# Four attention layers on one core: a new order of work, one product of 320 keys, smaller helpers

## The chip, the core and the metric

The kernel runs on one core of a Trainium2 chip. Its time is the device time of one execution in microseconds (us); of several runs the median is given. The core has five queues of instructions that run beside each other: TensorE (matrix products), VectorE, ScalarE, GpSimd and SyncE, which only issues transfers (DMAs). In the profile they are PE (PEld for its weight loads), DVE, ACT, POOL and SP. ScalarE's queue can issue DMAs too.

## The reference

2048 tokens of 512 values pass through four layers A, B, A, B. Each normalizes its input, projects it to queries, keys and values of 32 heads with 16 values each, attends, projects with `wo` and adds the input.

```python
# layer A: each token attends to 8 keys, 2 tokens apart
idx = pos[:, None] - (jnp.arange(8) * 2)[None, :]
logits = where(idx >= 0, einsum("bhsd,bhswd->bhsw", q, kg) * scale, -1e9)
o = einsum("bhsw,bhswd->bhsd", softmax(logits), vg)
# layer B: each token attends to the 256 tokens that end with itself
mask = (i - j >= 0) & (i - j < 256)
p = softmax(where(mask, einsum("bhqd,bhkd->bhqk", q, k) * scale, -1e9))
o = einsum("bhqk,bhkd->bhqd", p, v)
# between layers
x = x + A(layernorm(x)); x = x + B(layernorm(x)); ...   # twice
```

## The kernel before, in words

Tokens go through in 8 chunks of 256 per layer, and a chunk of a layer starts as soon as the chunk of the layer below has ended. Matrix products split float32 numbers into two halves of 16 bits (high and low) and add three products (L1037 to L1039 for products that come out transposed, L1057 to L1060 for the others).

**Weights.** `prep` loads each weight matrix, sums its squares, and forms a power of two as its scale: the sums are reduced over columns (`most`, L871), transposed by TensorE, reduced again and worked into factors on one partition (`one`, L880 to L886), and spread to 128 partitions by a second product (`spreads`, L893). ScalarE and VectorE then split the weights with it.

**Layer A.** Scores of the local window come from 128 small products (L1196), go to DRAM and back as bands (`shelve`, `band`), become weights by a softmax on VectorE, ScalarE and GpSimd, pass through DRAM again (`put`, `get` into `ptt`), and meet the values, which were read with a shift (`window`), in small products (L1305).

**Layer B.** Queries and keys are written to DRAM as high and low halves and read back into stacks, 48 partitions of high, low and high halves for two groups of heads (`stack`, L1358). `stk[hf, 0]` holds queries; `stk[hf, 1]` and `stk[hf, 2]` hold the keys of two chunks in turn. In every chunk but a layer's first, one step of `halves` (L1416) makes the scores of 128 queries of one column of heads against the 320 keys that can matter, for the row maxima: four positions in the array, and for each the keys of the chunk before (`bef`) and of this one (`now`) in a product of their own, 8 products and 8 weight loads. VectorE picks and reduces (L1435, L1431), the maxima go through DRAM into the query stack as two more rows (`mput`, `mget`), and the scores are formed again with keys as rows (L1567), raised by ScalarE (L1577, L1589), masked by GpSimd or VectorE (L1606, L1600) and multiplied with the values (L1622), which carry a column of ones so that the sum of the weights comes along. In all chunks but the last, the sums are gathered, inverted and spread by DMAs. In the last chunk (`final`), TensorE spreads each head group's sums over partitions (`across`, L1653), VectorE inverts 128×256 of them (L1657) and multiplies (L1658).

**The order.** Nothing here is left to run time. `plan.add` notes each task with an engine, a cost, what it reads and writes and, for some, another engine (`alt`). The table `ORDER` gives every task its place in its engine's queue; a negative entry puts it on the other engine. `Plan.order` merges the five queues into one program by its model of costs and delays, and so also chooses the memory banks of TensorE's results. The model holds a clock for TensorE (`RECENT`, `WARM`), a delay for its instruction supply (`SUPPLY`), and a price for leaving one kind of TensorE work for another (`mode`, `LEAVE`): F are projections, Q the steps of L1416 and L1567, X, V, C and R the other small products. 122 warm-up blocks of three products (L1752, scope "W") have places too. A queue runs in order: an instruction that waits holds up all behind it.

## Time and profile before

| | |
|---|---|
| Median of 3 runs | 1435.89 us (1431.45 to 1438.87) |
| The profiled execution's own time | 1437.16 us, span 1435.4 us |
| TensorE: busy, products | 1306.9 us, 28226 |
| VectorE, ScalarE, GpSimd: busy | 867.4, 824.0, 392.8 us |
| DMA: moved, packets | 195.20 MB, 185233 |

The span runs from the first to the last instruction. Busy time is the time in which at least one instruction of an engine is under way; products overlap, so a product's own duration is longer than its share of the engine. A row of waits reads: engine, line, what it waited for, then the total in us, the number of times and the longest. A row of a timeline reads: start, duration, engine, line, operation, number of instructions merged into it, and in brackets the idle time of that engine before it with what ended it. A row of a stretch of time gives for each engine its busy time and, in brackets, its number of instructions, then TensorE's granted clock (1.00 is full) and the busy share of the DMA engines.

### The profile page before, as it was taken

How to read it: one execution, taken by the hardware profiler on the slowest of the kernel's cores; microseconds unless marked ns; L12 is line 12 of the kernel's file. 1: busy time of each engine (PE TensorE's matmuls, PEld its weight loads, DVE VectorE, ACT ScalarE, POOL GpSimd, SP SyncE). 2: the span in 40 equal slices, each digit the busy share in tenths (PEclk: the TensorE clock that was granted, in tenths of full speed). 3: DMA queues.
4: the chain of work that ended last, by engine and by line, in shares of the span. 5: the costliest groups of instructions: out<-in, count | busy, mean ns of one | idle time of the engine just before them, and what ended most of it. 6: DMA issues, size and time to landing. Idle time of an engine off the chain costs nothing.

```text
span 1435.4 us, 64450 instructions
## 1 busy us (share of the span) xinstructions
PE 1306.9 (91%) x28226; PEld 861.9 (60%) x28226; DVE 867.4 (60%) x1942; ACT 824.0 (57%) x1298; POOL 392.8 (27%) x841
## 2 busy tenths in 40 slices
PE   9999999898999989989998989979988798998987
PEld 7775566574665747547564646647565474664643
DVE  5646764755657385555845548574753656658596
ACT  8555666374755656546583646637565364654643
POOL 4221232222432142132332322423323222212040
PEclk9999999899999999999999999989999899999999
DMA  9765555737355463645538364463636535354322
GB/s 301 210 169 143 139 112 153 160 99 170 84 167 125 125 161 98 156 119 146 117 103 191 97 189 130 149 149 97 157 78 175 122 110 158 85 154 109 103 61 68
DMA packets 185233, 195.20 MB, mean 136 GB/s; under 512 B 92892, under 2 KB 123356, under 8 KB 184952
## 3 DMA queue, kind: packets, MB, share of 16 engines
q1 hardware_dynamic: 155772, 163.27, 43.0%
q10 hardware_dynamic: 29180, 27.82, 7.5%
q8 instruction: 221, 3.62, 1.1%
q14 instruction: 60, 0.49, 0.1%
HBM read 94.11 MB, written 79.36 MB: 121 GB/s over the span
## 4 chain that ended last, share of the span: by engine, by line
PE 65%; DMA 12%; DVE 7%; issue 5%; ACT 4%; SPq 4%; ACTq 2%; POOL 1%; DVEq 0%; POOLq 0%
PE banks L1037 7%; PE banks L1622 7%; PE banks L1038 7%; PE banks L1039 6%; PE banks L1059 6%; PE banks L1057 6%; PE banks L1060 5%; PE banks L1567 4%; PE banks L1416 4%; PE banks L1305 3%; PE banks L1196 3%; DVE m L1431 2%; PE banks L1752 2%; DMA stk<-re 2%; DMA re<-eh 1%
## 5 line engine op out<-in xcount | busy, mean ns | idle before, releaser
L1431 DVE TENSOR_REDUCE m<-banks 128x2 f32<-128x512 f32 x448 | 302.0, 689 | 8.4
L1577 ACT ACTIVATE p<-banks,sclB 128x896 f32<-128x896 f32 x224 | 220.9, 1008 | 62.1 <-PE banks L1567 48.0
L1435 DVE COPY_PREDICATED banks<-trm,banks 128x128 f32<-128x128 int16 x448 | 124.5, 291 | 143.1 <-PE banks L1416 127.6
L1606 POOL TENSOR_SCALAR_AFFINE_SELECT p<-p 64x256 f32<-64x256 f32 x292 | 114.2, 413 | 277.8 <-ACT p L1577 262.8
L1606 POOL TENSOR_SCALAR_AFFINE_SELECT ps<-ps 64x256 f32<-64x256 f32 x280 | 109.7, 414 | 260.4 <-ACT ps L1589 219.0
L1416 PE MATMUL banks<-stk,stk 48*64 48x256 f16 (+3 forms) x3584 | 139.2, 246 | 36.3 <-DVE m L1431 10.0
L1416 PEld LDWEIGHTS <-stk 48*64 48x64 f16 x3584 | 79.0, 109 | 113.2 <-issue 95.8
L1567 PE MATMUL banks<-stk,stk 64*64 64x128 f16 (+3 forms) x3584 | 120.9, 242 | 20.4 <-DMA stk<-md 3.7
L1589 ACT ACTIVATE ps<-banks,sclB 128x768 f32<-128x768 f32 x112 | 100.5, 902 | 46.7 <-PE banks L1567 21.4
L1622 PE MATMUL banks<-p,v 64*32 64x192 f32 (+1 forms) x3584 | 114.8, 360 | 5.7 <-issue 1.6
L1567 PEld LDWEIGHTS <-stk 64*64 64x64 f16 x3584 | 70.7, 109 | 74.0 <-issue 64.1
L1337 DVE SCALAR_TENSOR_TENSOR el<-banks,eh 128x512 f16<-128x512 f32 x64 | 42.8, 689 | 99.9 <-ACT eh L1334 88.1
L1205 ACT COPY s<-banks 128x624 f32<-128x624 f32 x64 | 75.1, 1263 | 44.9 <-PE banks L1196 39.5
L1639 ACT COPY os<-banks 128x256 f32<-128x256 f32 x112 | 41.1, 375 | 81.2 <-PE banks L1622 62.8
L1636 DVE TENSOR_TENSOR os<-os,banks 128x256 f32<-128x256 f32 x112 | 45.8, 416 | 69.0 <-ACT os L1639 65.9
L1622 PEld LDWEIGHTS banks<-p,v 64*32 64x32 f32 x3584 | 65.4, 107 | 32.4 <-issue 16.0
L1622 PE MATMUL banks<-ps,v 64*32 64x64 f32 (+1 forms) x3584 | 69.2, 246 | 8.5 <-issue 8.5
L1305 PE MATMUL banks<-ptt,vs 39*32 39x64 f32 x4096 | 58.9, 247 | 17.7 <-DMA ptt<-ptd 6.8
L1037 PE MATMUL banks<-xh,wA0h 128*128 128x256 f16 x256 | 71.5, 279 | 1.8 <-DMA xh<-ht 1.8
L1622 PEld LDWEIGHTS banks<-ps,v 64*32 64x32 f32 x3584 | 64.6, 106 | 13.5 <-issue 12.0
L1037 PE MATMUL banks<-xh,wA1h 128*128 128x256 f16 x256 | 71.2, 278 | 0.4 <-DMA xh<-ht 0.2
L1038 PE MATMUL banks<-xl,wA0h 128*128 128x256 f16 x256 | 70.9, 277 | 0.0
(215 smaller groups left out, 3096.9 us busy)
## 6 DMA issues: line engine op xcount, KB each, us to landing
sd<-s SPq DMA_DIRECT2D x128, 156.0 KB
stk<-re SPq DMA_DIRECT2D x188, 96.0 KB
ptt<-ptd SPq DMA_DIRECT2D x124, 96.0 KB
re<-eh SPq DMA_DIRECT2D x80, 128.0 KB
vd<-ve SPq DMA_DIRECT2D x32, 256.0 KB
xm<-y SPq DMA_DIRECT2D x32, 256.0 KB
y<-xm SPq DMA_DIRECT2D x32, 256.0 KB
vs<-vd ACTq DMA_DIRECT2D x44, 156.0 KB
```

The costliest lines, as they stand in the source:

```text
L1037: nc.tensor.matmul(ps[mp].t[:, i], wh, xh, start=k == 0, stop=False)
L1038: nc.tensor.matmul(ps[mp].t[:, i], wh, xl, start=False, stop=False)
L1039: nc.tensor.matmul(ps[mp].t[:, i], wl, xh, start=False, stop=k == 3)
L1305: nc.tensor.matmul(acc.t[32 * r : 32 * r + 32, bb].rearrange("p (a x q u) -> p a x q u", a=2, q=16, u=2)[:, :, 2 * m + b2], vs.t[k, b2, 32 ...
L1416: nc.tensor.matmul(o, lhs, k, start=True, stop=True, tile_position=(64 * par, 64 * h))
L1431: nc.vector.tensor_reduce(out=m.t[:, :, u, qb], in_=ps.t[:, :, 0 : 2 * P], op=ALU.max, axis=AX.X)
L1435: nc.vector.copy_predicated(t[:, :, 0:64], trm[:, 0].bitcast(I16).unsqueeze(1).broadcast_to([P, 2, 64]), t[:, :, C : C + 64])
L1567: nc.tensor.matmul(ps.t[64 * h : 64 * h + 64, par, at + x0 : at + x0 + q1 - q0], stk[hf, kt][r, col, k0 : k0 + 64], stk[hf, 0][r, col, q0: ...
L1577: nc.scalar.activation(big.t[:, 2 * i : 2 * i + 2], ps.t[:, :, 0:448], AF.Exp, scale=scl["B", 1])
L1589: nc.scalar.activation(small.t.rearrange("p (i m) x -> p m i x", i=2), ps.t[:, :, 0:384].rearrange("p m (i x) -> p m i x", i=2), AF.Exp, s ...
L1606: E.affine_select(out=v, in_=v, pattern=[[0, 4], [a, 64]], compare_op=op, fill=0.0, base=0, channel_multiplier=-a)
L1622: nc.tensor.matmul(acc.t[32 * mm : 32 * mm + 32, h, q0:q1], vv[r, 17 * (H * blk + hd) : 17 * (H * blk + hd) + 32], x.t[r, mm, x0 : x0 + q1 ...
```

## The change

- All lists of `ORDER` are new. Few tasks keep their places. Counted over the lists, TensorE's queue changes its mode 1145 times (1011 before).
- The model of the planner: TensorE's clock is set by activity in four staggered grids of 3.4133 us, its activity numbers are others, `SUPPLY` and `SLACK` are larger and the supply is asked for one after the other, and some DMA costs are higher. The model reaches the program through the merging and the banks.
- `band`, `window`, `get`, `stack`, `mget` and `spread` have no other engine any more: 80 such issues leave ScalarE's queue. Of the others, ScalarE's queue takes 30 more net (`mput` 6, `gather` 6, `gather_o` 8, `shelve` 7, `put` 3). In all, its issues go from 181 to 131.
- By the lists, VectorE takes 90 masks (81), 10 subtractions `rest` (4), 10 scalings of `oc` (3) and 8 differences `less` (13).
- The key stacks of two chunks lie in one tile, `ring`, chunk beside chunk. In odd chunks the 320 keys lie in a row, and `halves` needs 4 products and 4 weight loads a step. In even chunks it has 8 as before. The transfers into key stacks now write pieces of 512 bytes; the DRAM tensor `re` has its axes in another order.
- The weight scale: the sums of squares are multiplied by a matrix of ones, so that each partition has their total, and five small VectorE operations make the factors in place. The scale comes from the total and not from the largest.
- The last chunk's division: products bring the sums to a tile of 128×8, VectorE inverts that, ScalarE spreads it, products turn it back, and VectorE multiplies from the bank.

```diff
-RECENT, WARM, EDGE = 3.4, 0.31, 0.05
-SLACK = 0.6, 0.25
-SUPPLY = 4.2
+GRID, LOW, EDGE = 3.4133, 0.4, 0.03
+SLACK = 0.9, 0.45
+SUPPLY = 5.0
...
-    stk, vst = {}, {}
+    stk, vst, ring = {}, {}, {}
     for hf in range(2):
+        stk[hf, 0] = cst.tile([P, 8, C], F16, name=f"stk{hf}_q")
+        ring[hf] = cst.tile([P, 8, 2, C], F16, name=f"stk{hf}_k")
         for i in range(3):
-            stk[hf, i] = cst.tile([P, 8, C], F16, name=f"stk{hf}_{i}")
+            if i:
+                stk[hf, i] = ring[hf][:, :, i - 1]
...
-            def most(am=am, ax=ax, n=n):
-                nc.vector.tensor_reduce(out=ax.t[:, 0:n], in_=am.t[:, 0:n], op=ALU.max, axis=AX.X)
...
-            plan.add("DVE", 1.0 if n == 1 else 1.2, one, r=[vpt], w=[va])
-            plan.add("PE", 0.3, spreads, r=[va, vone], w=[vpb])
...
+            def total(pt=pt, am=am, n=n):
+                for j in range(2):
+                    nc.tensor.matmul(pt.t[:, 0:n], ones.t.rearrange("p a b -> p (a b)")[:, 0:P], am.t[:, 0:n, j], start=j == 0, stop=j == 1)
+
+            plan.add("PE", 0.3, total, r=[*vam, vone], w=[vpt], rec=8)
+
+            def factors(some=some, pt=pt, a1=a1, n=n):
+                a, b = a1.t[:, 0:n], pscs[T, some]
+                nc.vector.tensor_scalar(a, pt.t[:, 0:n], 2.0 ** -120, 2.0 ** 120, op0=ALU.max, op1=ALU.min)
+                nc.vector.tensor_scalar(a.bitcast(I32), a.bitcast(I32), 1, 0x7F800000,
                                         op0=ALU.logical_shift_right, op1=ALU.bitwise_and)
+                nc.vector.tensor_scalar(b[:, :, 0], a, 2.0 ** 64, None, op0=ALU.mult)
+                nc.vector.tensor_scalar(a, a, 2.0 ** 64 / WS, None, op0=ALU.mult)
+                nc.vector.reciprocal(b[:, :, 1], a)
...
-            plan.add("SP", 2.15, shelve, r=vS, w=[vsd], size=600, alt=("ACT", 2.4))
-            plan.add("SP", 0.65, band, r=[vsd], w=[vL[t]], size=160, alt=("ACT", 0.7))
+            plan.add("SP", 2.4, shelve, r=vS, w=[vsd], size=600, alt=("ACT", 2.4))
+            plan.add("SP", 0.65, band, r=[vsd], w=[vL[t]], size=160)
...
                     for par in range(2):
-                        E.dma_start(t[64 * par : 64 * par + 48, 4 * hp : 4 * hp + 4].rearrange("p a t -> p (a t)"), src[j, par])
-
-                plan.add("SP", 1.3, stack, r=vre[0] + vre[1], w=[vst[hf, i, hp]], size=192, alt=("ACT", 1.35))
+                        x = t[64 * par : 64 * par + 48, 4 * hp : 4 * hp + 4]
+                        if s == 0:
+                            E.dma_start(x.rearrange("p a t -> p (a t)"), src[j, par])
+                        else:
+                            E.dma_start(x, src[j, par].rearrange("p (a t) -> p a t", a=4))
+
+                plan.add("SP", 1.3, stack, r=vre[0] + vre[1], w=[vst[hf, i, hp]], size=225 if s else 192)
...
-                        for part in range(2):
+                        for part in range(2 - c % 2):
                             for h in range(2):
                                 for par in range(2):
                                     r = slice(64 * par, 64 * par + 48)
                                     n = C - qb * P - 64 * h
                                     lhs = stk[hf, 0][r, col, qb * P + 64 * h : qb * P + 64 * h + 64]
                                     o = ps.t[64 * h : 64 * h + 64, par, 0:320]
-                                    o, k = (o[:, 0:n], stk[hf, bef][r, col, C - n :]) if part == 0 else (o[:, n:], stk[hf, now][r, col, : 320 - n])
+                                    if c % 2:
+                                        k = ring[hf][r, col].rearrange("p i t -> p (i t)")[:, C - n : C - n + 320]
+                                    else:
+                                        o, k = (o[:, 0:n], stk[hf, bef][r, col, C - n :]) if part == 0 else (o[:, n:], stk[hf, now][r, col, : 320 - n])
                                     nc.tensor.matmul(o, lhs, k, start=True, stop=True, tile_position=(64 * par, 64 * h))
...
-                def divide(pb=pb, sh=sh, some=some):
-                    nc.vector.reciprocal(sh.t[:, 0:C], pb.t[:, 0:C])
-                    nc.vector.tensor_mul(some(), some(), sh.t[:, 0:C])
...
+                def sums(pb=pb, some=some):
+                    for b in range(2):
+                        nc.tensor.matmul(pb.t[:, C + 4 * b : C + 4 * b + 4], some()[:, b * P : (b + 1) * P], idf[:, 16::32], start=True, stop=True)
+
+                def wide(r8=r8, sh=sh):
+                    nc.scalar.copy(sh.t[:, 0:C].rearrange("p (b m x) -> p b m x", b=2, m=4),
+                                   r8.t.rearrange("p (b m) -> p b m", b=2).unsqueeze(3).broadcast_to([P, 2, 4, 32]))
+
+                def back(pb=pb, sh=sh):
+                    for b in range(2):
+                        nc.tensor.matmul(pb.t[:, b * P : (b + 1) * P], sh.t[:, b * P : (b + 1) * P], idf, start=True, stop=True)
+
+                plan.add("PE", 0.3, sums, r=[vsm], w=[vps], mode="F", act=0.02, rec=8)
+                plan.add("DVE", 0.16, lambda pb=pb, r8=r8: nc.vector.reciprocal(r8.t, pb.t[:, C : C + 8]), r=[vps], w=[vr8])
+                plan.add("ACT", 0.3, wide, r=[vr8], w=[vbr])
+                plan.add("PE", 0.47, back, r=[vbr], w=[vpb], mode="F", act=0.42, rec=8)
```

More of the change, by code (lines that the diff above doesn't have):

```diff
@@ L568, in order, with cool @@
         slow, at, rest = None, 0.0, 0.0
-        dma, mode, tail, use, since = 0.0, "", "", 0.0, 0.0
-        n, asked, told = 3, 0.0, 0.0
+        dma, mode = 0.0, ""
+        heat = [[0.0, GRID * (k + 1) / 4, 0.0] for k in range(4)]
+        n, asked, told, mark = 3, 0.0, 0.0, 0.0
         out = []
+        def cool(h):
+            h[2] = 1.0 / (1.0 + math.exp((h[0] / GRID - LOW) / EDGE))
+            h[0] = 0.0
+            h[1] += GRID
         def begins(e):
@@ L634, in order @@
                 mode = t.mode
-                use *= math.exp((since - now) / RECENT)
-                clock = 0.5 + 0.5 / (1.0 + math.exp((WARM - use) / EDGE))
-                a = t.act / us * clock
-                us /= clock
+                for h in heat:
+                    while h[1] <= now:
+                        cool(h)
+                us /= 1.0 - sum(h[2] for h in heat) / 8
                 wait = 0.0
                 for x in range(n + 1, n + t.rec + 1):
-                    if x % 256 == 140:
-                        asked, told = told, now + wait + us * (x - n) / t.rec
+                    if x % 256 == 152:
+                        mark = now + wait + us * (x - n) / t.rec
+                    elif x % 256 == 168:
+                        asked, told = told, max(mark, now, told + SUPPLY if told else 0.0)
                     elif x % 256 == 193 and x > 256:
@@ L646, in order @@
                 us += wait
-                use = a + (use - a) * math.exp(-us / RECENT)
-                since = now + us
+                for h in heat:
+                    while h[1] <= now + us:
+                        h[0] += t.act * (h[1] - max(now, h[1] - GRID)) / us
+                        cool(h)
+                    h[0] += t.act * (now + us - max(now, h[1] - GRID)) / us
             elif e == "POOL":
@@ L780 @@
     plan.begin("S")
-    plan.add("POOL", 0.3, lambda: nc.gpsimd.memset(ones.t[0:4, 0, 0:P], 1.0), w=[vone])
+    plan.add("POOL", 0.3, lambda: nc.gpsimd.memset(ones.t[:, 0, 0:P], 1.0), w=[vone])
     plan.add("POOL", 1.8, lambda: nc.gpsimd.memset(ptt, 0.0), w=[vptt])
@@ L902, in prep @@
+            plan.add("DVE", 0.7, factors, r=[vpt], w=[va, vsc])
             for s in some:
@@ L1542, in layer_b @@
                         nxt = Val(acc)
-                        plan.add("PE", 0.67, values, r=[vp2, *vvt[(c - 1 + b) % 3], *([chain] if chain else [])], w=[vacc, nxt], mode="C", act=0.16, rec=32)
+                        plan.add("PE", 0.67, values, r=[vp2, *vvt[(c - 1 + b) % 3], *([chain] if chain else [])], w=[vacc, nxt], mode="C", act=0.64, rec=32)
                         chain = nxt
@@ L1648, in layer_b @@
                 pb = Banks(psum, 1, [P, D])
[L1649 to L1661 removed]
+                r8 = buf("psm", [P, 8], F32, "r8", f"r8{hh}")
+                vps, vpb, vr8 = Val(pb), Val(pb), Val(r8)
+                def sums(pb=pb, some=some):
[11 more added lines that the diff above has]
+                plan.add("PE", 0.47, back, r=[vbr], w=[vpb], mode="F", act=0.42, rec=8)
+                plan.add("DVE", 0.36, lambda pb=pb, some=some: nc.vector.tensor_mul(some(), some(), pb.t[:, 0:C]), r=[vpb, vsm], w=[vos[hf][hp]])
             if not final:
@@ L1701, in layer_b, with spread @@
         vbc = Val(os_[1])
[L1703 removed]
+        def spread(E=nc.sync):
             E.dma_start(flat(os_[1]), scr.t.unsqueeze(0).broadcast_to([16, 8, 4 * C]))
[L1706 removed]
+        plan.add("SP", 0.55, spread, r=[vscr, *vog], w=[vbc], size=840)
         vo = [[], []]
```

72 lines of the change are left out of this document (21 added, 51 removed), and 794 rows, old and new, of the table ORDER.

## The prediction

> **What bounds the kernel now.** I read the page first, then the waits of TensorE, then the trace around its longest waits.
>
> ```profile
> PE 1306.9 (91%) x28226; PEld 861.9 (60%) x28226; DVE 867.4 (60%) x1942; ACT 824.0 (57%) x1298; POOL 392.8 (27%) x841
> q1 hardware_dynamic: 155772, 163.27, 43.0%
> q8 instruction: 221, 3.62, 1.1%
> ...
> core 0: 1435.4 us, clock 0.958
> ```
>
> TensorE is busy for 1306.9 of 1435.4 us, so 128.5 us are idle, and its clock is below full for some of the rest (0.958 in the mean). No other engine is near it. Only what shortens TensorE's instruction stream or its stops can move the end. The waits of TensorE, longest first in total, tell what the stops are:
>
> ```profile
> PE banks L1196 <- issue: 11.6, 8, 2.3
> PE banks L1622 <- issue: 10.1, 9, 1.6
> PE banks L1416 <- DVE m L1431: 10.0, 25, 0.8
> PE banks L1416 <- DMA stk<-re: 8.2, 6, 2.6
> PE banks L1305 <- DMA ptt<-ptd: 6.8, 7, 1.8
> PE banks L1416 <- issue: 6.5, 6, 2.8
> PE banks L1305 <- ACT v L1368: 5.5, 1, 5.5
> PE banks L1305 <- issue: 5.1, 3, 2.6
> ...
> PE banks L1567 <- DMA stk<-md: 3.7, 6, 1.4
> PE banks L1567 <- DVE m L1431: 3.6, 8, 0.9
> ...
> PE banks L1567 <- issue: 2.3, 3, 1.2
> ```
>
> The five rows with "issue" sum to 35.6 us in 29 stops: TensorE stood still and waited for nothing that the profile shows. Three views say what it was. First the longest such stop in order of time, then stretches of time from one such stop to the next, with the busy time of each engine and the number of its instructions in brackets:
>
> ```profile
> 1142.37 0.24 PE L1416 MATMUL banks<-stk,stk 48*64 48x128 f16 x4
> 1145.44 0.70 PE L1416 MATMUL banks<-stk,stk 48*64 48x192 f16 x12 [2.82 <-issue]
> 1146.07 0.61 PE L1059 MATMUL banks<-wA3h,oh 128*128 128x512 f16 x1
> 1146.47 0.63 PE L1060 MATMUL banks<-wA3l,oh 128*128 128x512 f16 x1
> ```
>
> ```profile
> 1059.13:1093.53 34.40, 33.70 (x766) 24.77 (x766) 13.01 (x22) 24.18 (x38) 11.05 (x23) 0.95 0.37 102
> 1093.53:1145.43 51.90, 40.57 (x892) 22.70 (x891) 30.39 (x66) 22.79 (x37) 17.57 (x37) 0.89 0.59 149
> 1137.00:1142.60 5.60, 5.60 (x236) 3.85 (x235) 4.22 (x10) 4.93 (x10) 3.75 (x9) 1.00 0.47 100
> 1145.40:1148.90 3.50, 3.46 (x22) 1.30 (x26) 1.42 (x4) 0.00 (x0) 0.67 (x1) 0.50 0.02 5
> ```
>
> TensorE stops with four of the eight products of one step done; no semaphore stands in the middle of a step. From stop to stop it runs 766+766 = 1532 and 892+891 = 1783 instructions, that is 6 and 7 times 255. The page's instruction queue moves 221 packets of 16.4 KB for 2×28226 instructions, 255 each. I read these stops as TensorE running out of instructions: 471 of them went by in the 5.6 us before this one. And a stop has a second price: the next 3.5 us run at a clock of 0.50, 1.75 us lost for 2.82 us stopped, 0.6 of its length.
>
> **The parts, and the sum.** It is made against the profiled execution's own 1437.2 us (span 1435.4 and 1.8 around it), which lies 1.3 us above the median of the runs. All counts are from the order lists and the code of the diff.
>
> *Mode switches.* In TensorE's new order, work of one mode gives way to another 1145 times, not 1011: 134 more, mostly because attention scores stand alone or in twos between projections. A step between projections shows the price, and three steps together how long one is:
>
> ```profile
> 709.64 0.61 PE L1416 MATMUL banks<-stk,stk 48*64 48x256 f16 x24
> 710.19 0.28 PE L1037 MATMUL banks<-xh,wA0h 128*128 128x256 f16 x1
> ...
> 711.29 0.27 PE L1038 MATMUL banks<-xl,wA0h 128*128 128x256 f16 x1
> 711.40 0.27 PE L1039 MATMUL banks<-xh,wA0l 128*128 128x256 f16 x1
> 711.61 0.34 PE L1416 MATMUL banks<-stk,stk 48*64 48x128 f16 x8
> 711.87 0.28 PE L1037 MATMUL banks<-xh,wA1h 128*128 128x256 f16 x1
> ```
>
> A projection product takes 0.11 us (711.29 to 711.40). The next step starts 0.21 us after the last of them, so entering costs 0.10. Three steps and a leaving take 0.55 us, one step and a leaving 0.26: a step is 0.145 to 0.15 us, a leaving 0.11. So 134 switches cost 13.4 us; nothing where TensorE would have waited anyway. I take **+13** (0 to +13.4).
>
> *Product of 320 keys.* The 8 odd chunks have 32 steps each; 256 steps become 4 products instead of 8, with half the weight loads. The columns streamed stay 320; at 0.11 us for 256 they need 0.1375 us. From 0.15 that leaves at most 0.0125 × 256 = 3.2 us. I take **−1.5** (−3.2 to 0).
>
> *Instruction supply.* 1024 products and as many loads fewer are 2048 of 56452 instructions, 8 of 221 packets. In proportion that is 8/221 × 35.6 = 1.3 us. But these steps also ask for instructions at half the rate, and the finer order puts slow-asking projections (two instructions in 0.11 us, against 16 in 0.15) between fast-asking work; that is what the switches buy. Bounds: all 35.6 gone, or 3.6 (a tenth) more where dense work falls together elsewhere. I take **−11**, a third, for the supply itself is unchanged.
>
> *DMA issues leave ScalarE.* 80 issues that wait for another transfer's landing (stacks 34, windows 22, the maximum's rows 14, bands 6, and 4 more) go from ScalarE's queue to SyncE's for good; 30 of other kinds net come the other way (gathers, shelving, puts), which wait for compute engines. What such an issue does to a queue that must also compute:
>
> ```profile
> 1126.89 0.71 ACTq L1473 DMA_DIRECT2D stk<-md  x2
> 1127.65 0.60 ACT L1368 ACTIVATE v<-banks 128x512 f32<-128x512 f32 x1 [12.12 <-DMA stk<-md]
> 1128.30 2.13 PE L1305 MATMUL banks<-ptt,vs 39*32 39x64 f32 x128 [5.52 <-ACT v L1368]
> ```
>
> ScalarE computed nothing for 12.12 us, and TensorE lost 5.52 behind it. I take **−4** (−5.5 to 0).
>
> *SyncE's queue and the 512-byte pieces.* SyncE gains 50 issues net. Behind each that waits stand stores and loads of other stages, whose readers wait too. The key stacks now go to SBUF in 192 pieces of 512 bytes instead of 48 of 2 KB: 128 issues, 18432 packets more. At q1's mean (0.43 × 16 × 1435 us / 155772 = 63 ns per packet) an issue takes 0.6 us longer over 16 engines. TensorE's rows with a DMA sum to 18.7 us. Bounds: unchanged, or doubled with 0.6 us for each of the six stack stops on top, +22.3. I take **+3**: the transfers are not late in most steps today, since only 19 stops in all have these three rows. That both stacks share a tile costs nothing more: every step after a layer's first chunk reads both halves, so even if the halves were guarded as one, a write would wait for reads that it waits for today.
>
> *VectorE as the freer of banks.* TensorE waits 13.6 us for the maxima (L1431) to free banks. With scores in smaller lots between projections, less of this is left; against it nine masks, six subtractions and seven scalings more stand on VectorE, taken from GpSimd, and five differences fewer; it is 60% busy. I take **−5** (−13.6 to +13.6).
>
> *The last chunk.* The reciprocal of 128×256 becomes one of 128×8, spread by a ScalarE copy and two transposing products:
>
> ```profile
> 1417.45 1.76 DVE L1657 RECIPROCAL sh<-banks 128x256 f32<-128x256 f32 x1 [0.19 <-PE banks L1653]
> ...
> 1421.37 0.43 DVE L1658 TENSOR_TENSOR os<-os,sh 128x256 f32<-128x256 f32 x1
> ...
> 11.79 0.14 DVE L886 RECIPROCAL a1A<-a1A 1x1 f32<-1x1 f32 x1
> ...
> 1384.00:1422.00 38.00, 30.02 (x740) 17.33 (x729) 33.09 (x53) 18.91 (x26) 12.63 (x27) 0.96 0.13 35
> ```
>
> In these 38 us VectorE is busy for 33.1 (87%), TensorE for 30.0: here VectorE leads. Eight reciprocals give back about 8 × (1.76 − 0.14) = 13 us, with the small one priced by the row of the smallest in this trace. TensorE stands next, 8 us lower, and takes one more step per head, entered and left for 0.21 us: 1.7 us. The last pair alone (1417.45 to 1421.8) would go reciprocal, copy, product, two multiplications: an estimated 2.5 us instead of 4.35. Bounds −9.5 to −1.8; I take **−6.5**.
>
> *Weight scales by ones.* Two product round trips and a reduction leave the chain of the first weights, some 1.5 us of it. But the first projection comes right behind warm-up products:
>
> ```profile
> 16.22 0.82 PE L1752 MATMUL banks<-idf 128*128 128x256 f16 x6
> 16.87 0.27 PE L1037 MATMUL banks<-xh,wA0h 128*128 128x256 f16 x1
> ```
>
> Six products of 0.11 us from 16.22 end at 16.87. The new order has the same 38 warm-up blocks ahead of the first projection and only one small step fewer, so **−0.5** (−0.7 to 0): the cover is the warm-up itself.
>
> *Clock.* The stops fall by 11 + 4 + 5 − 3 = 17 us. Not every stop is followed by a slow stretch; at half of the 0.6 that is **−5** (−10 to 0).
>
> The Trainium skill ("TensorE: Matmul & The Clock Gate", Part 1) asks for an idle window of about 3.4 us before the clock halves. Here 2.82 us were enough. By that rule the clock term would be near 0, and the sum 5 us higher.
>
> Sum: 13 − 1.5 − 11 − 4 + 3 − 5 − 6.5 − 0.5 − 5 = −17.5, so 1437.2 → 1419.7 in its own profiled run, and 1.3 less, **1418 us**, for the median.
>
> **Rivals.**
>
> *More comes of the order.* The supply term reaches −20, banks −9, and the clock the full 0.6 of 30 us: −18. With the rest as above −43.5, **1392**. For it: the 29 stops have one cause, and the new order can be laid around it. Against: 13 us of switches come first.
>
> *The supply stops only move.* Supply −1.3 and clock −2: −4.8, **1431**, no change. For it: 213 packets still have to come, and the dense lots (values, the local scores of layer A) are as dense as before. Against: L1416's own 6.5 us lie partly in odd chunks. The Trainium skill ("Runtime: NRT & Kernel Launch", Instruction fetch mechanics) has blocks of 256 instructions, which agrees with 255 per stop, but holds that fetching is hidden by dispatch; by that rule there would be nothing to gain here, and the rows with 2.82 us speak against it.
>
> *SyncE's queue becomes the bound.* The following rows are the waits of SyncE's queue on landings:
>
> ```profile
> SPq L1473 <- DMA md<-mt: 33.9, 27, 4.1
> ...
> SPq L1288 <- DMA vs<-vd: 16.7, 7, 5.1
> ```
>
> A mean stop of 1.3 and 2.4 us holds all that is queued behind. With 80 more issues of this kind, TensorE's DMA stops double: +22.3 instead of +3. The stops then grow by 2.3 in all, the clock term turns to +1.4, and the sum is +8.2: **1444**, slower. It decides from about 17 us of added DMA stops. Against: ScalarE's queue held the same waits, and computing behind them.
>
> **How the numbers follow.** About 0.5% (7 us) is what a measurement of this kernel tells from no change. Forecast 0.47, more 0.20, only moved 0.17, SyncE 0.14; 0.02 is left. The first two are faster, and a fifth of the third: 0.70. The rest of the third and the remainder give 0.16 for the same, the last 0.14 for slower. The likeliest's own range is 1405 to 1430; the range goes from 1390, just under the second case, to 1446, just over the last.
>
> **What would show it.** "Issue" stops of TensorE near 25 us, none inside an odd chunk's scores; no row of ScalarE waiting on a stack or a window; switches still 0.10 us; steps of odd chunks at 0.14 to 0.15 us; VectorE below TensorE in the last 50 us; the first projection near 16.4. The forecast fails if stops behind DMAs pass 35 us, or if the "issue" stops stay above 33.

## The result and the profile after

The changed kernel takes 1455.22 us in the median of 4 runs (1450.96 to 1458.31), beside 1435.81 us for the kernel before: a ratio of 1.0135, 95% interval 1.0098 to 1.0173. Every ratio here leaves out slow runs, those more than 1.5% above the fastest of the same kernel. The changed kernel is slower, and it lies above the forecast of 1418 us and above its whole range. Its profiled execution took 1450.96 us, 13.8 us more than that of before.

The rows of its page that answer to the first ones shown of before are the busy times and the DMA queues; the view of the cores has span and clock.

```profile
PE 1319.0 (91%) x27206; PEld 844.3 (58%) x27206; DVE 863.3 (60%) x1945; ACT 824.9 (57%) x1304; POOL 380.6 (26%) x800
...
q1 hardware_dynamic: 177264, 172.63, 43.9%
...
q8 instruction: 213, 3.49, 1.1%
```

```profile
core 0: 1449.2 us, clock 0.967
```

TensorE has 1020 products fewer in the records, yet it is busy 12.1 us longer, although its clock is better (0.967 against 0.958). Busy time times mean clock is a rough measure of the work as it would take at full clock: 1306.9 × 0.958 = 1252.0 us before, 1319.0 × 0.967 = 1275.5 us after. The changed kernel gives TensorE's array some 23 us more to do.

The trace allows the same split more exactly. From the start of one product to the start of the next, time is idle, or work at full clock, or work at half clock, of which half counts as lost:

```
                       idle   lost to half clock   work at full clock     first to last start
kernel before         123.6        54.5                1251.7                 1429.9
changed kernel        125.3        44.3                1274.1                 1443.7
difference             +1.7       -10.2                 +22.4                  +13.9
```

So 22.4 us of work came in, 10.2 us of slow clock went, and the idle time, which was to fall by 17 us, did not fall at all. What it is made of, in TensorE's waits of the changed kernel:

```profile
PE banks L1624 <- issue: 25.5, 13, 3.6
PE banks L1418 <- DVE m L1433: 7.7, 21, 1.0
PE banks L1418 <- DMA stk_q<-re: 5.9, 8, 1.5
PE banks L1569 <- DVE m L1433: 5.4, 13, 0.8
PE banks L1569 <- issue: 5.3, 3, 3.5
...
PE banks L1569 <- DMA stk_q<-md: 4.8, 3, 3.4
...
PE banks L1300 <- issue: 4.0, 4, 1.1
...
PE banks L1191 <- issue: 3.0, 1, 3.0
...
PE banks L1418 <- issue: 1.3, 1, 1.3
```

Summed over all rows of this view, before and after: issue 39.5 to 49.3 us, VectorE 30.5 to 23.1, DMA 21.0 to 14.6, ScalarE 27.4 to 33.6. What was to shrink most grew. It also moved: the values (L1624) stop 25.5 us for instructions, where their line L1622 of before had 10.1; the local scores and the maxima fell from 11.6 and 6.5 to 3.0 and 1.3.

### The profile page after: what moved, and what is told of

It reads as the page before. It is cut to its first block, busy times and chain, and to the rows that moved or that the text cites. A ratio compares the mean times of both kernels' runs of the same rounds, so it can differ in the third digit from the quotient of the medians.

```text
span 1449.2 us, 62327 instructions
## 1 busy us (share of the span) xinstructions
PE 1319.0 (91%) x27206; PEld 844.3 (58%) x27206; DVE 863.3 (60%) x1945; ACT 824.9 (57%) x1304; POOL 380.6 (26%) x800
## 4 chain that ended last, share of the span: by engine, by line
PE 59%; DMA 10%; ACT 7%; DVE 6%; issue 6%; SPq 4%; ACTq 2%; POOL 0%; DVEq 0%; POOLq 0%
PE banks L1624 7%; PE banks L1032 7%; PE banks L1033 6%; PE banks L1034 6%; PE banks L1054 6%; PE banks L1052 5%; PE banks L1055 5%; PE banks L1418 5%; PE banks L1569 5%; PE banks L1300 3%; DVE m L1433 2%; PE banks L1191 2%; ACT p L1579 2%; DMA ptt<-ptd 1%; SPq L1342 1%
## 5 line engine op out<-in xcount | busy, mean ns | idle before, releaser
L1608 POOL TENSOR_SCALAR_AFFINE_SELECT p<-p 64x256 f32<-64x256 f32 x272 | 106.7, 414 | 353.5 <-ACT p L1579 318.3
L1418 PE MATMUL banks<-stk_k,stk_q 48*64 48x320 f16 (+4 forms) x2560 | 139.6, 273 | 27.5 <-DVE m L1433 7.7
L1569 PE MATMUL banks<-stk_q,stk_k 64*64 64x256 f16 (+3 forms) x3584 | 121.4, 242 | 29.6 <-DVE m L1433 5.4
L1608 POOL TENSOR_SCALAR_AFFINE_SELECT ps<-ps 64x256 f32<-64x256 f32 x264 | 104.0, 416 | 163.3 <-ACT ps L1591 158.8
L1624 PE MATMUL banks<-p,v 64*32 64x192 f32 (+1 forms) x3584 | 119.5, 364 | 17.8 <-issue 15.0
L1418 PEld LDWEIGHTS <-stk_q 48*64 48x64 f16 x2560 | 64.1, 107 | 118.9 <-issue 103.2
L1569 PEld LDWEIGHTS <-stk_k 64*64 64x64 f16 x3584 | 71.6, 109 | 90.0 <-issue 73.5
L1624 PEld LDWEIGHTS banks<-p,v 64*32 64x32 f32 x3584 | 63.7, 108 | 48.0 <-issue 26.2
L1624 PE MATMUL banks<-ps,v 64*32 64x64 f32 (+1 forms) x3584 | 70.0, 250 | 10.5 <-issue 10.4
L1624 PEld LDWEIGHTS banks<-ps,v 64*32 64x32 f32 x3584 | 63.7, 107 | 19.0 <-issue 16.8
L1034 PE MATMUL banks<-xh,wA0l 128*128 128x256 f16 x256 | 71.3, 278 | 0.8 <-issue 0.8
L1033 PE MATMUL banks<-xl,wA1h 128*128 128x256 f16 x256 | 71.5, 279 | 0.0
```

What stands on the lines that cost most here:

```text
L1033: nc.tensor.matmul(ps[mp].t[:, i], wh, xl, start=False, stop=False)
L1034: nc.tensor.matmul(ps[mp].t[:, i], wl, xh, start=False, stop=k == 3)
L1418: nc.tensor.matmul(o, lhs, k, start=True, stop=True, tile_position=(64 * par, 64 * h))
L1569: nc.tensor.matmul(ps.t[64 * h : 64 * h + 64, par, at + x0 : at + x0 + q1 - q0], stk[hf, kt][r, col, k0 : k0 + 64], stk[hf, 0][r, col, q0: ...
L1608: E.affine_select(out=v, in_=v, pattern=[[0, 4], [a, 64]], compare_op=op, fill=0.0, base=0, channel_multiplier=-a)
L1624: nc.tensor.matmul(acc.t[32 * mm : 32 * mm + 32, h, q0:q1], vv[r, 17 * (H * blk + hd) : 17 * (H * blk + hd) + 32], x.t[r, mm, x0 : x0 + q1 ...
```

## The experiments

Ratios are to the kernel before, run beside each on the same chip, with 95% intervals. The runs went to several chips, so across groups it is the ratios that are compared. 18 kernels ran.

### The parts that are not order, in the order of before

The first run has the ring tile, the 512-byte pieces and the product of 320 keys, and nothing else:

```diff
-                        for part in range(2):
+                        for part in range(2 - c % 2):
...
-                                    o, k = (o[:, 0:n], stk[hf, bef][r, col, C - n :]) if part == 0 else (o[:, n:], stk[hf, now][r, col, : 320 - n])
+                                    if c % 2:
+                                        k = ring[hf][r, col].rearrange("p i t -> p (i t)")[:, C - n : C - n + 320]
```

> The kernel before with the ring of key stacks and the product of 320 keys alone, pieces of 512 bytes included; order as before. In the trace of after a step of four products takes 160 ns against 162 of a step of eight, so 256 steps give 0.5 us; 2048 instructions fewer to supply are 8 of 221 packets, 1.5 us. Order theory: 0 to 3 us faster, 1433 to 1436. Pieces theory: 5 to 10 us slower, and TensorE's stops behind stacks grow from 8 us.

Measured: 1441.03 us, ratio 1.0001 (0.996 to 1.0041). The second adds the small reciprocal and the weight scales, as in the change:

> The kernel before with the code parts of the change alone: key stacks of two chunks in one tile with the product of 320 keys on odd chunks, the small reciprocal, the weight scales by ones. The order lists, the planner's model and the queues of the DMA issues stay those of before; the added tasks of the last chunk are put in between. If the loss comes from the new order (its 134 switches, and stops that it doesn't save), the code parts are worth something by themselves: 5 to 10 us faster than before, 1426 to 1431. If it comes from the pieces of 512 bytes, this kernel is slower too: 1440 to 1450. If the parts do nothing, 1436.

Measured: 1438.78 us, ratio 0.9978 (0.9942 to 1.0015). A third, run later, has only the reciprocal and the scales:

> The kernel before with two parts of the change alone, the small reciprocal of the last chunk and the weight scales by ones, in the order of before. The run with these and the product of 320 keys took 59.4 us from the 60th finished half row block to the end, before 62.4, so 3 us are to be had at the end and near none at the start: ratio 0.996 to 0.999. If the small reciprocal lies beside other work: 0.999 to 1.002.

Measured: 1441.39 us, ratio 0.9996 (0.9969 to 1.0024). So none of these parts can be told from no change in the order of before. The loss must come with the new order, or with a part and the order together. The product alone did one thing that counted later. Its waits:

```profile
PE banks L1632 <- issue: 22.0, 14, 3.0
PE banks L1308 <- DMA ptt<-ptd: 12.0, 14, 3.1
PE banks L1199 <- issue: 9.5, 8, 2.6
PE banks L1308 <- issue: 8.6, 6, 2.2
```

L1632 is the values' line here: with 2048 entries fewer in TensorE's list, in unchanged order, the values' stops for instructions went from 10.1 to 22.0 us, as in the changed kernel. All its rows with "issue" sum to 47.8 us, 8.3 more than before, and still its time is that of before: in its profiled execution some 5 us less went to half clock and VectorE's rows were 2.9 us shorter. So a larger sum of stops need not show in the time.

### Parts of the order, in the kernel before

Three runs take one property of the new order each. In the first, 51 pairs of tiled steps (T) between untiled work (U) are pulled apart:

```
before:  U T T U U        this run:  U T U T U        (1011 changes of tiling become 1113)
```

> The kernel before with 51 steps of scores moved behind the projection piece that follows them, so that pairs stand apart: 102 switches of TensorE's mode more (1113), nothing else. If a switch costs 0.10 us on the path and buys nothing, 10 us slower, about 1446. If the waits hide the switches or the finer mix saves stops, within 3 us of before.

Measured: 1457.82 us, ratio 1.011 (1.0054 to 1.0167), 15.2 us above the median of before on that chip, 1442.66. Busy time times clock rises to 1323.1 × 0.959 = 1268.9 us, by 16.9 us, 0.166 us for each of the 102 changes. The rows, from the page and the view of the cores:

```profile
PE 1323.1 (91%) x28226; PEld 862.3 (59%) x28226; DVE 871.2 (60%) x1942; ACT 825.4 (57%) x1298; POOL 394.2 (27%) x841
```

```profile
core 0: 1457.1 us, clock 0.959
```

In the second, the 80 issues go from ScalarE's queue to SyncE's, each put ahead of the first SyncE task that the plan of before starts after it:

```diff
-  "A0": [... 33, 25, -40, 90, 89, ...]      (negative: on ScalarE's queue, place 39)
+  "A0": [... 33, 25, 27.5, 90, 89, ...]
```

> The kernel before with the 80 issues that after moves from ScalarE's queue to SyncE's for good (stacks, windows, maxima rows, bands, spreads, one get), each put where the planner of before starts it. If SyncE's queue is the cause of the loss, 10 to 25 us slower with more stops of TensorE behind DMAs than the 20 us of before. If ScalarE's freedom is worth what I forecast, 4 us faster; switch theory: within 5 us.

Measured: 1467.51 us, ratio 1.0179 (1.0111 to 1.0248). Moved without a new order around them, these issues do make SyncE's queue the bound: TensorE's stops behind DMAs rise from 21.0 to 38.8 us, with these rows ahead:

```profile
PE banks L1309 <- DMA ptt<-ptd: 16.1, 16, 5.0
...
PE banks L1571 <- DMA stk<-md: 6.8, 6, 3.1
```

But in the changed kernel they are 14.6 us. The rival has a real mechanism, and it is not what happened. The third leaves all lists as they are and merges them under the new model, so that only banks and buffers are dealt out otherwise:

```diff
-RECENT, WARM, EDGE = 3.4, 0.31, 0.05
-SLACK = 0.6, 0.25
-SUPPLY = 4.2
+GRID, LOW, EDGE = 3.4133, 0.4, 0.03
+SLACK = 0.9, 0.45
+SUPPLY = 5.0
```

> The kernel before with its own instructions, lists and queues, but the five lists are merged under the changed kernel's constants and clock model, which alters only which banks and buffers each value is given and so what a step waits for. If the new model's banks and buffers are what costs, this alone is slower by 5 us or more (ratio above 1.004). If the changes of tiling cost (1011, as before), it is within 3 us of before: 0.998 to 1.002.

Measured: 1476.18 us, ratio 1.0247 (1.0199 to 1.0296). This spoke for banks: TensorE's stops behind ScalarE rose from 27.4 to 51.0 us and behind VectorE from 30.5 to 46.8. An order and the model that deals out its banks belong together; this one was never meant for the new model. In the changed kernel, where they do belong together, VectorE's rows fell to 23.1 and ScalarE's rose to 33.6, in sum 56.7 us where before had 57.9, so banks do not account for its loss either.

### Fewer changes of tiling

If the 134 extra changes of tiling are what the changed kernel pays for, taking some out should pay. The same swap was made the other way round in the changed kernel, wherever it could be (1063 changes instead of 1145), and then only where it did not lengthen the planner's schedule (1089); and in the kernel before with all parts that are not order (958 instead of 1006):

```
changed kernel:  U T U T        these runs:  U U T T
```

> The changed kernel, with TensorE's list alone altered: where a tiled step stood alone between untiled ones and the next tiled step came at most three steps later, it is put beside that one. TensorE changes its array tiling 1063 times instead of 1145; same instructions, queues, tiles and costs. If the changes of tiling are what the change paid for, 82 fewer at 0.10 us (the row difference in the trace of before) to 0.15 us (15.2 us for 102 in the run that only split pairs) give back 8 to 12 us: 5 to 11 us over the kernel before, ratio 1.004 to 1.008. If it is waits of the new order (banks, ScalarE, stacks), nothing comes back or they grow, since steps now come later than planned: ratio 1.012 to 1.02.

> As the run before it, but only those steps are put together whose later place does not lengthen the planner's own schedule: 1089 changes of tiling instead of 1145. By the changes of tiling 56 x 0.10 to 0.15 = 5.6 to 8.4 us come back: ratio 1.007 to 1.010. By waits of the order: as the changed kernel, 1.0135.

> The parts of the change that are not order (one ring tile for the stacks, the product of 320 keys, the small reciprocal, the weight scales by ones), in the order of before, and TensorE's list of that with neighbouring tiled steps put together: 958 changes of tiling instead of 1006. By the changes of tiling: 4.8 to 7.2 us below the run of those parts alone (ratio 0.998), so ratio 0.993 to 0.995, 1429 to 1433 us where before takes 1439. If steps that come later than planned cost as much in waits for banks and for ScalarE as the switches give back: 0.997 to 1.003.

Measured: 1466.01 us, ratio 1.0173 (1.013 to 1.0217); 1458.87 us, 1.0112 (1.0078 to 1.0146); 1448.07 us, 1.0049 (1.0019 to 1.0079). None is faster than what it started from. The last is slower (it started from 0.9978), and the first two cannot be told from the changed kernel's 1.0135, though 8 to 12 us and 6 to 8 us were to come back. In the first the array work did fall a little, by 4.3 us in the split from start to start, but in its profiled execution the idle time was 18 us more: VectorE's rows went from 23.1 to 32.7 us, ScalarE's from 33.6 to 42.3. The theory that the changes of tiling decide found no support here. Each of these runs also puts other work together into one stretch of TensorE's list, which turns out below to matter by itself, so they do not price the changes of tiling cleanly.

### The product taken back, in the new order

The changed kernel with two products on odd chunks again:

```diff
-                        for part in range(2 - c % 2):
+                        for part in range(2):
```

> The changed kernel, but odd chunks too take their maxima step in two products as before (128 groups of four instructions more), all else as in the changed kernel. If the steps that end in a product of 320 columns give back at their end what they save inside (leaving a tiled step cost 0.138 us in the kernel before, 0.160 in the changed one, going from one tiled group to the next 0.095 and 0.114; the tiled products themselves took 14.6 us less), the time stays that of the changed kernel within 4 us: ratio 1.011 to 1.016, and the chip's time for leaving falls back to near 0.138 us. If the product is what moved the instruction stops to the values (10.1 us in the kernel before, 22.0 with the product alone, 25.5 in the changed kernel), they fall below 15 us there and some 5 us turn up at the maxima steps. If the product is a gain of its own: slower by more than 4 us, ratio over 1.017.

Measured: 1441.37 us, ratio 0.9987 (0.9953 to 1.0021). The whole loss is gone, though the time was expected to stay within 4 us of the changed kernel. What took it away is an edit that had cost and gained nothing in the order of before, and that gives TensorE more instructions. Its waits:

```profile
PE banks L1622 <- issue: 7.4, 4, 2.7
...
PE banks L1416 <- issue: 6.2, 5, 1.6
```

The stops for instructions fall from 49.3 to 24.9 us, with those of the values from 25.5 to 7.4. The array work stays at 1274.1 us by the split from start to start. What the expectation said about the end of a step is right: the times below are from the starts of consecutive products at full clock, idle time taken out, with the number of places and the mean price beyond an ordinary product.

```
                            entering tiled work    leaving it
kernel before                416    0.095 us       416    0.138 us
product alone (old order)    416    0.096 us       416    0.155 us
changed kernel               480    0.096 us       480    0.160 us
two products (new order)     480    0.095 us       480    0.138 us
```

A step of 320-column products saves time inside and gives it back when it is left: from the start of the last product of a step to the next projection it is 0.128 us in the median after 64 columns, 0.184 after 192 and 0.252 after 320. So the array work, the same with and without the loss, is not its reason. What fell together with the loss are the stops for instructions, by 24.4 us, while ScalarE's rows grew by 10.9. For these stops two causes were left: the product itself makes such stops, or its 2048 missing entries only change where the blocks of TensorE's list end.

### The list shifted, nothing else changed

In the first warm-up blocks, three products of 256 columns become six of 128. That is the same array time, and 6 entries more (product and weight load) for each warm-up block so treated, ahead of the first projection. 11, 22, 33 and 42 blocks make 66, 132, 198 and 252 entries, about a quarter, a half, three quarters and a whole of a block of 256.

```diff
-            for _ in range(3):
-                nc.tensor.matmul(junk.t[:, 0 : 2 * P], v[:, 0:P], v, start=True, stop=True)
+            n = 6 if early else 3
+            for _ in range(n):
+                nc.tensor.matmul(junk.t[:, 0 : 6 * P // n], v[:, 0:P], v[:, 0 : 6 * P // n], start=True, stop=True)
```

The changed kernel, in the order of the shift:

> As the run before it with 11 blocks, 66 entries, a quarter of a block. By where the blocks end: issue stops differ from both 49.3 us and those of the run with 132 entries. By the product as such: 45 to 53 us and ratio 1.012 to 1.015.

> The changed kernel; in the first 22 warm-up blocks three products of 256 columns are six of 128, so that TensorE's instruction list is 132 entries longer ahead of the first projection, at the same array time; all that follows is the same, half a block of some 255 instructions further on. If the changed kernel loses because its blocks happen to end inside the values, the stops on issue (49.3 us, 25.5 of them at the values) move: they differ by 10 us or more and the time with them, ratio anywhere from 0.998 to 1.018. If the product of 320 keys as such makes the stops, wherever the blocks end: issue 45 to 53 us, ratio 1.012 to 1.015.

> The changed kernel with 198 entries ahead (33 blocks), three quarters of a block. By where the blocks end: between the runs with 132 and with 252, issue 25 to 50 us, ratio 0.985 to 1.013. By something that grows with the list: 0.983 or below.

> The changed kernel with 252 entries ahead (42 blocks), nearly one whole block of 256 (213 packets of 16384 bytes hold 27206 products at two entries of 64 bytes each). By where the blocks end, the stops come back to the places and the size of the changed kernel: issue 44 to 54 us, above 15 us of it at the values, ratio 1.008 to 1.017. If the 132 entries helped by something else that grows with the list (a longer or warmer start, say), the ratio stays at 0.99 or below.

The changed kernel with two products, and the kernel before:

> The changed kernel with two products on odd chunks (ratio 0.999, issue stops 24.9 us), its list 132 entries longer ahead of the first projection. By where the blocks end: stops grow by 8 us or more, ratio 1.004 or above. By the product as such: stops stay under 30 us, ratio 0.997 to 1.002.

> The kernel before with 66 entries ahead, a quarter of a block. By where the blocks end: issue between 35 and 55 us, ratio 0.99 to 1.02; with 0, 132 and 198 entries it gives a mean over the four quarters, to set beside that of the changed kernel. By something that grows with the list: 1.008 to 1.012, half of the run with 132.

> The kernel before with its list 132 entries longer ahead of the first projection. By where the blocks end: issue stops leave 39.5 us by 8 us or more in either direction and the time moves by more than 4 us. By the product as such: no change, ratio 0.998 to 1.002.

> The kernel before with 198 entries ahead, three quarters of a block. By where the blocks end: between 132 entries (1.020) and none (1.000) or outside both. By something that grows with the list: 1.03.

Measured, as ratios to the unshifted kernel before, with the stops for instructions of the profiled execution:

```
entries ahead     changed kernel                         kernel before
  0            1.0135 (1.0098 to 1.0173)   49.3 us      1                            39.5 us
 66            1.0097 (1.0061 to 1.0132)   51.2 us      1.0150 (1.0086 to 1.0215)      -
132            0.9830 (0.9794 to 0.9866)   24.7 us      1.0203 (1.0164 to 1.0242)    48.8 us
198            0.9856 (0.9801 to 0.9910)   20.7 us      1.0034 (1.0000 to 1.0068)    33.4 us
252            1.0126 (1.0079 to 1.0173)   41.5 us
two products, 132 entries ahead: 0.9994 (0.9968 to 1.0020), 35.8 us
```

The sum marked - is not compared: that profiled execution took 1472.91 us, the second longest of its six. Some ranges were missed. With 132 entries ahead the changed kernel gained more than expected (0.9830, below 0.998 to 1.018); the sums of 20.7 and 41.5 us lie just below 25 to 50 and 44 to 54; and with 66 the sum is near that of no shift, though its stops stand at other work (20.1 us at the value mix, 4.0 without a shift). With 252 entries 16.6 us stand at the values again.

Apart from the split warm-up products, the same instructions in the same order on the same data move by 3% when the list slides by half a block, and they come back when it slides by nearly a whole one. Nothing that grows with the list does that. One passage shows it at the level of single products: 32 value products, 128 products of the value mix (L1300), 32 value products. In the changed kernel:

```profile
541.36 0.56 PE L1624 MATMUL banks<-ps,v 64*32 64x128 f32 x32
541.71 1.66 PE L1300 MATMUL banks<-ptt,vs 39*32 39x64 f32 x128
543.15 0.99 PE L1624 MATMUL banks<-p,v 64*32 64x256 f32 x31
547.74 0.48 PE L1624 MATMUL banks<-p,v 64*32 64x192 f32 x1 [3.60 <-issue]
```

With 252 entries ahead:

```profile
541.04 1.70 PE L1300 MATMUL banks<-ptt,vs 39*32 39x64 f32 x128
542.52 1.03 PE L1624 MATMUL banks<-p,v 64*32 64x256 f32 x32
543.48 0.32 PE L1418 MATMUL banks<-stk_k,stk_q 48*64 48x320 f16 x1
546.95 0.48 PE L1418 MATMUL banks<-stk_k,stk_q 48*64 48x320 f16 x3 [3.15 <-issue]
```

With 66 and with 132 entries ahead:

```profile
556.82 1.79 PE L1300 MATMUL banks<-ptt,vs 39*32 39x64 f32 x127
561.82 0.31 PE L1300 MATMUL banks<-ptt,vs 39*32 39x64 f32 x1 [3.22 <-issue]
```

```profile
550.11 1.33 PE L1300 MATMUL banks<-ptt,vs 39*32 39x64 f32 x94
552.83 0.55 PE L1300 MATMUL banks<-ptt,vs 39*32 39x64 f32 x34 [1.39 <-issue]
553.17 1.07 PE L1624 MATMUL banks<-p,v 64*32 64x256 f32 x32
```

Counted from the first product of the mix, the stop comes after 128 + 31 = 159 products, after 127, after 94, and, at 252 entries, after 128 + 32 + 1 = 161. A product has two entries, so the stops moved by 64 and 130 entries towards the start of the list, and by 4 towards its end, which is 256 − 252. Shifts of 66, 132 and 252 should do just that, to within one product. TensorE's list comes in blocks of 256 entries, and the stop stands at the end of a block, wherever that falls. The whole traces say the same: ahead of each of the 33 stops for instructions of the kernel before and the 31 of the changed kernel, the products and weight loads started so far number 193 or 194 more than a multiple of 256. In the four shifted runs of the changed kernel 101 of 105 stops stand there, within one entry. With 198 entries ahead, the end should fall some 60 products into the mix, and there the passage runs through without any stop:

```profile
534.21 1.83 PE L1300 MATMUL banks<-ptt,vs 39*32 39x64 f32 x128
535.82 0.99 PE L1624 MATMUL banks<-p,v 64*32 64x256 f32 x32
```

The best of these is faster than both kernels: the changed kernel with 132 entries ahead takes 1417.58 us, where the kernel before took 1442.73 on the same chip. From its page and the view of its cores:

```profile
PE 1308.7 (92%) x27272; PEld 843.6 (60%) x27272; DVE 864.5 (61%) x1945; ACT 823.4 (58%) x1304; POOL 380.4 (27%) x800
```

```profile
core 0: 1416.5 us, clock 0.976
```

Its array work is that of the changed kernel (1275.7 us from start to start); its idle time is 22.4 us less (its stops for instructions alone are 24.6 us less), and 11.8 us less are lost to half clock.

One run does not fit in: with two products and 132 entries ahead, the stops grew from 24.9 to 35.8 us, and the median stayed where it was (1441.84 beside 1441.37). The time is in the range of the product as such (0.997 to 1.002), the stops are not (under 30 us). ScalarE's rows fell by 9.9 us in the same profile (44.5 to 34.6), so other waits can take up what a stop leaves or adds.

Nor do sums of such stops give the time by themselves. Two products without a shift, and the changed kernel with 132 entries ahead, stop for 24.9 and 24.7 us, with ratios of 0.9987 and 0.9830; in the second, the profiled execution has 9.0 us less idle time in all and 8.6 us less lost to half clock. So it is shown that the place of the block ends moves the stops, and that in these two orders it moves the time by 2 to 3%. How much of that time goes through the stops themselves, and how much through the waits and the clock that change with them, is not shown.

How long a stop is follows from two times in each trace: when the block before is used up, and when the packet of 16384 bytes that brings the next one (queue q8) lands. For the five passages, in us:

```
entries ahead   block before:          packet of the next block:   first entry    stop
                first to last entry    starts       lands          of the next
  0             542.11 to 543.82       545.16       546.29         547.74         3.60
 66             556.81 to 558.38       559.16       560.38         561.82         3.22
132             549.76 to 551.22       550.34       551.37         552.83         1.39
252             541.47 to 543.48       544.24       545.55         546.95         3.15
198             530.50 to 534.97       531.07       532.03         534.97         none
```

The four stops end 1.40 to 1.46 us after the landing, and all 31 of the changed kernel 1.19 to 1.61 us after one. The packet starts 1.0 us after the first entry of the block before in the median, so a block that is soon used up runs out: of 41 blocks of the changed kernel that took under 4 us, 30 ended in such a stop, of the other 171 one did. But the density of the block does not set the length. The quickest of the four blocks (1.46 us) has the shortest stop, because its packet started 0.6 us after the block's first entry, and the others' 2.4 to 3.1 us after. Why a packet starts early or late stays open. Nor was it tried to place the ends by rearranging the list instead of lengthening it.

## Why the prediction was wrong, by its steps

**Instruction supply (−11, bounds −35.6 to +3.6; measured +9.8): the step that failed.** The prediction read the stops rightly as TensorE running out of instructions, and it counted the blocks (255 entries by its count). Then it took the stops as a property of how densely the work asks, which a finer order and fewer instructions must relieve. The stops do stand behind blocks that are soon used up, but which blocks those are depends on where the ends fall, and removing 2048 entries spread over the run moves all later ends. That the list gets shorter said nothing about the sign. At 132 and 198 entries ahead the same kernel has 24.7 and 20.7 us of these stops, 14.8 and 18.8 us below before: the relief that was forecast is in the new order, and it was there to be had or lost by a shift that no part of the change mentions. The upper bound of a tenth more was far too tight: the kernel before alone spans 33.4 to 48.8 us over three positions, the changed one 20.7 to 51.2. The Trainium skill ("Runtime: NRT & Kernel Launch", Instruction fetch mechanics) has the block of 256, which the four passages bear out to the product, and holds that fetching hides behind dispatch; the rows with 3.60 and 3.22 us and the 3% between positions disagree.

**Its rival "the supply stops only move"** was right in kind, since they went to the values as it said, but it priced the move at no change, 1431. They moved and grew.

**Mode switches (+13, bounds 0 to +13.4; measured about +15 to +18).** The measured array work rose by 22.4 us. The last chunk's extra products take 3.4 of it, and the product of 320 keys 1.4 (its run alone, 1253.1 against 1251.7). The rest, 17.6, is left for 64 more entrances and 64 more exits, 0.14 us each; at 0.095 and 0.138 us they come to 14.9, and what the other 2.7 are is not shown. The entrance was priced well (0.10; 0.095), the exit was not (0.11; 0.138, and 0.160 in the mean where steps of 320 columns are among them). As the bounds had no room above 13.4, they were wrong.

**Product of 320 keys (−1.5; no gain).** The step inside a run takes 160 ns instead of 162 in the median, and what is saved on weight loads is paid at the exit. In time, 1.0001.

**DMA issues and SyncE's queue (−4 and +3; −6.4 behind DMAs, +6.2 behind ScalarE).** TensorE's stops behind DMAs fell instead of growing, and the 512-byte pieces cost nothing measurable. "No row of ScalarE waiting on a stack" did not come true; these rows are from ScalarE's waits in the changed kernel, beside long ones on the gathers that came to its queue:

```profile
ACT v L1367 <- DMA oc<-os: 14.0, 2, 11.1
ACT p L1579 <- DMA rc<-os: 13.6, 2, 10.5
...
ACT ht L994 <- DMA stk_k<-re: 8.3, 1, 8.3
```

**VectorE as the freer of banks (−5; −7.4 over all its rows).** The size is near, the reason is not: the rows of the maxima went from 13.6 to 13.1 only.

**The last chunk (−6.5).** From the 60th of the 64 finished half row blocks to the end it took 62.4 us before, 58.9 with this part and the scales in the old order, 47.2 in the changed kernel. The reciprocal fell from 1.76 to 0.21 us, as this group of the changed kernel shows:

```profile
L1667 DVE RECIPROCAL r<-banks 128x8 f32<-128x8 f32 x8 | 1.7, 207 | 1.4 <-PE banks L1656 1.3
```

In the old order the whole run gained nothing from it that can be measured (0.9996); 3.5 us at its place is what can be said. The rest of the 15.2 us came with the new order. VectorE did fall below TensorE at the end, as forecast: 33.9 against 42.8 us busy in the last 50, where before had 35.2 against 36.2.

**Weight scales (−0.5; none).** The first projection starts at 16.91 us, where before it was 16.87. The warm-up is the cover, as said.

**Clock (−5; −10.2).** More than forecast, though the stops did not get shorter in sum. The price behind it was read too low. The stretch that was shown ends at 1148.90, but the clock stayed at 0.50 until 1151.40, as this row with TensorE's busy time and clock shows:

```profile
1145.44:1151.40 5.96, 5.96 (x47) 0.50 0.01 3
```

That is 3.0 us lost behind the stop of 2.82 us, as much as its length and not 0.6 of it.

**The sum.** −17.5 us was forecast, +13.8 measured in the profiled execution. Averaged over the four positions 0, 66, 132 and 198, the changed kernel stands at 0.998 and the kernel before at 1.010. Their quotient is 0.988, some 17 us of 1440. As a mean over positions, which is an estimate from four points each, the forecast was close, but that is luck: it knew nothing of positions, and its terms were off one by one. For the one position in which the change was made it had the wrong sign. The kernel before stood at or near its best position of the four, the changed one at or near its worst.

## What to carry to other kernels

When a kernel's engine stops for "issue" in the middle of a step, find the length of the blocks of its list and note where they end, before reading anything into a change that alters the number of instructions: here a shift by half a block was worth 3%, more than the whole change. Compare two versions at several shifts of the list (a few split warm-up products are enough), and take the best shift as the last step of tuning. Runs of one part at a time can mislead in such a kernel, since each of them also moves the ends of the blocks or the banks.

## What the runs showed of the hardware that was not expected

- The ends of TensorE's instruction blocks stand at fixed entries of its list, 256 apart. The stop there was anything from nothing to 3.6 us in the same passage as the list was shifted.
- Such a stop ends 1.2 to 1.6 us after the 16384 bytes of the next block have landed, in all 31 stops of the changed kernel and all 33 of the kernel before.
- What stops for instructions cost differs. Between the unshifted changed kernel and the one with 132 entries ahead, 24.6 us of such stops went with 32.7 us of time, 1450.96 to 1418.27 us; the rest is mostly clock (0.967 to 0.976). With two products 24.4 us went with 17.5 (1433.47 us), and the product alone in the old order added 8.3 us of stops and 0.5 us of time (1437.69 beside 1437.16).
- In these traces entering tiled work costs 0.095 us and leaving it 0.138 us, and 0.16 us in the mean with the steps of 320 columns among them. Fewer and longer products did not help the steps of odd chunks (1.0001 in the old order).
